# A new written-out order of instructions for a three-part float32 kernel on one core

## The chip, the cores and the metric

The kernel runs on one core of one Trainium2 chip. The metric is the device time of one execution in microseconds (us), given as the median of several runs. Five instruction streams matter: PE (TensorE, matmuls), DVE (VectorE), ACT (ScalarE), POOL (GpSimd), and SP (SyncE), which issues every DMA of this kernel. Each works through its own row of instructions strictly in the order of that row, and waits where an instruction needs something that another stream has not finished.

## What is computed

The reference is local attention with block summaries, followed by two gated feed-forward layers without a residual:

```python
def _attn_ref(q, k, v):                      # (2, 8, 768, 64) each
    k_sum = k.reshape(B, H, nb, 32, D).max(axis=3)
    v_sum = v.reshape(B, H, nb, 32, D).mean(axis=3)
    ...                                      # a window of 16 to either side, and 24 summaries
    return np.matmul(a, v_all)

def _moe_ref(x, w1, w2, w3, w_out):          # x: 1536 x 512, d_ff 1024
    h = (x @ w1) * (x @ w2) @ w3
    return h @ w_out

def _moe2_ref(x, w_in, w_out):               # d_ff 2048
    h = x @ w_in
    g = h * np.clip(h + 3.0, 0.0, 6.0) / 6.0
    return g @ w_out
```

The feed-forward weights arrive as 64-bit floats. The kernel rebuilds 32-bit floats from their two halves on the chip, and splits each into a high and a low part, so that one product of float32 accuracy is three matmuls (high by high, low by high, high by low).

## The kernel before

The work is a graph of 1997 numbered operations, built in `build` (L247). An operation is a load or store on SP, one instruction on DVE, ACT or POOL (the softmax's `inv` is three), or a group of matmuls on PE. Most copies and subtractions may run on either of two engines (`alt`, L71). Nothing decides this at run time: the table `PLAN` (L105) writes out, for PE, ACT, DVE, POOL and SP, which operations the engine does and in which order, and `Graph.in_order` (L88) only checks that the five lists together are possible and records them.

The stages, in the order of time:

- W' (`wprime`): w3 times w_out, once, so that the first layer's last two products become one. It has 16 steps. A step loads one or two tiles of 128x512 numbers (512 KB, `load`, L321), turns them into floats (`to_f32`: ACT L362, ACT L368 or DVE L371, DVE L376), splits them (`to_hi_lo`: a copy at L328 or L330, a subtraction at L387 on POOL or DVE), and gives PE four products of three matmuls each (`products`, L426), one into each of four PSUM banks. The tiles of the first step come in two halves of 128x256. The first tiles of attention (`probabilities`, `attend`, L531 to L640), and the sums over blocks (`first_k` L443, `first_v` L479, `vsum_rows` L505), are woven in. The loads of this stage go to the buffers raw0 to raw7, k to kres, q to qst, v windows to vall.
- The first layer (`ab`, `acc1`) in three blocks of 512 tokens, with the rest of attention woven in. At its side the weights w1 and w2 are converted, and later the second layer's output weights are converted and spilled to DRAM (`wo`).
- The second layer. Its first product is done by a seven-product scheme of 2x2 blocks (`half_product`, `added`, `gated`) in eight groups, with sums and differences of weights made on DVE, POOL and ACT (L826, L882, L387, L652). Sums of output weights are spilled to DRAM (`ws`).
- The last stage. Seven products of the same scheme over eight chunks each: every chunk loads 256 KB of `wo` or `ws` into half of a slot w20 to w27 (L1095), makes the high and low part of a difference of activations, and gives two products into two banks. Finished rows go from a bank through c0 to c3 to the output (L703, L1073).

A product into one bank is the chain

```python
for lhs, rhs in terms:
    for a, c in PASSES:                # L425: high*high, low*high, high*low
        nc.tensor.matmul(out=out_ap, lhsT=lhs(a), rhs=rhs(c), ...)
```

A buffer is used again as soon as its last reader is done. So an operation waits for its inputs, for the readers of the buffer that it writes, and for whatever stands before it in its engine's row.

Of the kernel before, what the change touches and what calls it, by code (L numbers as in the profile page):

```python
# [60 lines left out]
class Graph:  # L61
# [26 lines left out]
    def in_order(self, plan):  # L88
# [18 lines left out]
        33, 34, 35, 32, 49, 51, 50, 48, 58, 263, 73, 72, 74, 75, 274, 91, 89, 88, 90, 105, 106, 107, 104, 284,  # L107
        282, 122, 123, 120, 121, 286, 137, 138, 139, 292, 136, 300, 302, 153, 154, 155, 152, 304, 173, 171,
        181, 170, 183, 310, 180, 191, 318, 172, 320, 182, 192, 190, 322, 193, 200, 202, 201, 203, 210, 211,
        450, 212, 213, 458, 220, 230, 223, 460, 222, 232, 242, 462, 221, 231, 240, 241, 233, 243, 466, 465,  # L110
        475, 490, 491, 497, 485, 501, 483, 500, 496, 487, 506, 534, 540, 535, 510, 544, 519, 499, 509, 529,
        498, 508, 542, 527, 507, 541, 551, 531, 550, 552, 545, 562, 543, 553, 570, 578, 572, 577, 574, 587,
        584, 585, 586, 583, 601, 594, 593, 609, 596, 611, 595, 588, 616, 617, 625, 623, 622, 624, 613, 635,
        633, 634, 632, 627, 626, 648, 663, 670, 671, 664, 658, 673, 674, 669, 656, 681, 679, 703, 708, 710,
        680, 709, 672, 682, 711, 702, 660, 712, 687, 719, 718, 721, 695, 713, 697, 720, 742, 750, 749, 747,
        699, 748, 741, 726, 751, 736, 758, 759, 752, 757, 734, 768, 763, 738, 776, 769, 761, 774, 775, 765,
        760, 784, 786, 785, 777, 787, 778, 779, 796, 797, 806, 802, 805, 803, 804, 814, 812, 813, 807, 815,
        816, 817, 826, 825, 822, 836, 823, 824, 846, 834, 827, 832, 835, 837, 842, 845, 844, 847, 856, 855,
        854, 1051, 852, 857, 1066, 833, 843, 1072, 1053, 865, 864, 1057, 1083, 1092, 862, 1054, 1056, 1155,
        853, 863, 1055, 1145, 1068, 1078, 1153, 1147, 1087, 1163, 1162, 1161, 1173, 1160, 1148, 1170, 1171,  # L120
        1172, 1159, 1223, 1177, 1237, 1236, 1169, 1235, 1182, 1238, 1221, 1231, 1229, 1299, 1239, 1224, 1258,
        1248, 1246, 1247, 1307, 1253, 1249, 1314, 1313, 1300, 1324, 1245, 1312, 1322, 1297, 1329, 1388, 1305,
        1323, 1389, 1315, 1311, 1321, 1325, 1387, 1390, 1334, 1373, 1383, 1397, 1398, 1399, 1400, 1381, 1376,
        1391, 1451, 1375, 1401, 1405, 1464, 1463, 1449, 1465, 1466, 1410, 1457, 1459, 1467, 1527, 1452, 1475,
        1474, 1473, 1476, 1477, 1481, 1542, 1541, 1539, 1525, 1540, 1528, 1552, 1533, 1551, 1549, 1550, 1486,
        1598, 1595, 1535, 1543, 1596, 1597, 1553, 1562, 1583, 1581, 1557, 1591, 1589, 1584, 1607, 1599, 1606,
        1667, 1609, 1672, 1677, 1613, 1625, 1624, 1682, 1687, 1608, 1626, 1709, 1605, 1623, 1714, 1618, 1719,
        1666, 1708, 1713, 1718, 1630, 1629, 1723, 1728, 1733, 1628, 1671, 1676, 1738, 1681, 1686, 1691, 1696,
        1701, 1754, 1760, 1801, 1724, 1766, 1772, 1778, 1807, 1729, 1734, 1739, 1627, 1692, 1697, 1702, 1813,
# [1074 lines left out]
```

## Time and profile before

| | us |
|---|---|
| median of 3 runs | 554.68 |
| lowest and highest | 553.05, 556.45 |
| profiled execution | 554.5 |
| its span, first to last instruction | 552.7 |
| PE busy within the span | 531.0 |

The profile is one execution. Its span leaves out what lies around the instructions. An engine is counted busy while an instruction is in it; "<-" behind idle time names what ended it. Matmuls overlap in the pipeline, and their ends are modelled, so that the distance from start to start is what to read. PEclk is the granted share of TensorE's clock, 1.00 being 2.4 GHz.

### The profile page before, as it was taken

To read this page: it belongs to the slowest core of one execution; us is meant where nothing else is said; L and a number is where in the kernel's file an instruction comes from. 1 tells how busy PE (TensorE), PEld (TensorE's weight loads), DVE (VectorE), ACT (ScalarE), POOL (GpSimd) and SP (SyncE) were. 2 spreads that over 40 slices of the span, in tenths; PEclk is the share of its full clock that TensorE was granted. 3 is DMA by queue.
4 is the path that set the end of the run, shared out by engine and by line. 5 is a ranking of instruction groups with operands and counts; after the bars stand their busy time and mean duration, and the time that the engine had idled before them with its cause. 6 is when DMAs were issued, how large, how long until landed. Compare 5 with 4: busy or idle time off the path is not lost.

```text
span 552.7 us, 8430 instructions
## 1 busy us (share of the span) xinstructions
PE 531.0 (96%) x3112; PEld 430.2 (78%) x3112; DVE 437.3 (79%) x647; ACT 219.8 (40%) x365; POOL 259.7 (47%) x204
## 2 busy tenths in 40 slices
PE   2799999999999999999999999999999999999997
PEld 1477788877887877888788888888888888877885
DVE  5989999688989265497558898788989999867881
ACT  3598584273564321211425335534420352332231
POOL 0487377713521111174656235864654335656461
PEclk9999999999999999999999999999999999999999
DMA  8999597486679620001147674644653589758741
GB/s 311 399 341 326 154 320 270 128 288 195 212 265 303 242 80 30 0 1 39 42 169 236 195 272 163 219 165 132 269 177 114 196 296 377 259 167 267 234 147 57
DMA packets 54512, 111.32 MB, mean 201 GB/s; under 512 B 4792, under 2 KB 26296, under 8 KB 54472
## 3 DMA queue, kind: packets, MB, share of 16 engines
q1 hardware_dynamic: 54472, 110.79, 59.2%
q8 instruction: 24, 0.39, 0.3%
q14 instruction: 16, 0.13, 0.1%
HBM read 84.26 MB, written 26.21 MB: 200 GB/s over the span
## 4 chain that ended last, share of the span: by engine, by line
PE 81%; DVE 8%; DMA 4%; ACT 3%; POOL 2%; issue 1%; SPq 0%; DVEq 0%; POOLq 0%
PE bank L426 76%; PE bank L619 2%; PE bank L560 2%; DMA w<-ws 2%; PE bank L607 2%; DVE c L376 1%; DMA arena<-wo 1%; DMA raw<-in_wp_dram 1%; ACT bank L362 1%; ACT arena L328 1%; ACT raw L368 1%; DVE c L826 1%; POOL arena L652 1%; DVE arena L387 0%; DVE sc L570 0%
## 5 line engine op out<-in xcount | busy, mean ns | idle before, releaser
L426 PE MATMUL bank<-arena,w 128*128 128x512 f32 x1152 | 272.3, 390 | 1.9 <-DMA w<-ws 1.8
L426 PE MATMUL bank<-arena 128*128 128x512 f32 x960 | 242.3, 400 | 15.2 <-DVE arena L330 11.5
L426 PEld LDWEIGHTS bank<-arena,w 128*128 128x128 f32 x1152 | 215.2, 188 | 48.7 <-DVE arena L387 1.5
L426 PEld LDWEIGHTS bank<-arena 128*128 128x128 f32 x960 | 179.5, 191 | 56.6 <-DVE arena L330 10.8
L387 POOL TENSOR_TENSOR arena<-late_f,arena 128x512 fp32r<-128x512 f32 x28 | 39.3, 1406 | 43.9 <-ACT arena L328 16.3
L376 DVE SCALAR_TENSOR_TENSOR c<-c,raw 128x512 uint32<-128x512 uint32 x48 | 44.2, 930 | 8.5 <-ACT raw L368 7.7
L362 ACT ACTIVATE c<-raw 128x512 f32<-128x512 f32 x48 | 32.2, 674 | 44.8 <-DMA raw<-in_w_dram 36.7
L652 POOL TENSOR_TENSOR arena<-tg,arena 128x512 fp32r<-128x512 f32 x18 | 27.3, 1519 | 45.7 <-ACT arena L328 22.9
L387 POOL TENSOR_TENSOR arena<-c,arena 128x512 fp32r<-128x512 f32 (+1 forms) x25 | 32.6, 1319 | 29.6 <-DVE arena L330 16.1
L328 ACT ACTIVATE arena<-late_f 128x512 fp32r<-128x512 f32 x40 | 24.8, 628 | 51.6 <-DVE late_f L826 21.4
L387 DVE TENSOR_TENSOR arena<-late_f,arena 128x512 fp32r<-128x512 f32 x36 | 36.5, 1024 | 4.7 <-ACT arena L328 4.6
L587 POOL TENSOR_TENSOR sc<-sc,st 128x960 f32<-128x960 f32 x10 | 18.4, 1838 | 44.7 <-DVE st L584 44.7
L387 POOL TENSOR_TENSOR w<-c,w 128x512 fp32r<-128x512 f32 x17 | 25.0, 1474 | 16.8 <-ACT w L328 10.2
L368 ACT ACTIVATE raw<-raw 128x512 uint32<-128x512 uint32 (+1 forms) x46 | 30.0, 657 | 0.0
L328 ACT ACTIVATE w<-c 128x512 fp32r<-128x512 f32 x24 | 15.0, 630 | 32.9 <-PE bank L426 24.7
L669 DVE TENSOR_TENSOR tg<-ta,bank 128x512 f32<-128x512 f32 x24 | 16.3, 680 | 13.2 <-PE bank L426 6.1
L328 ACT ACTIVATE arena<-bank 128x512 fp32r<-128x512 f32 x27 | 15.7, 597 | 25.4 <-PE bank L426 16.2
L882 POOL TENSOR_TENSOR late_f<-arena 128x512 f32<-128x512 f32 x10 | 15.3, 1537 | 20.2 <-DMA arena<-wo 19.4
L387 POOL TENSOR_TENSOR raw<-c,raw 128x512 fp32r<-128x512 f32 x11 | 14.7, 1347 | 18.7 <-ACT raw L328 12.3
L826 POOL TENSOR_TENSOR late_f<-late_f,late_f 128x256 f32<-128x256 f32 (+1 forms) x14 | 15.6, 1116 | 15.4 <-DVE late_f L882 6.3
L376 DVE SCALAR_TENSOR_TENSOR c<-bank,raw 128x512 uint32<-128x512 uint32 (+1 forms) x26 | 16.6, 645 | 6.8 <-ACT raw L368 4.8
L371 DVE TENSOR_SCALAR raw<-raw 128x512 uint32<-128x512 uint32 (+1 forms) x28 | 15.7, 563 | 7.8 <-DMA raw<-in_w_dram 6.5
(88 smaller groups left out, 619.0 us busy)
## 6 DMA issues: line engine op xcount, KB each, us to landing
raw<-in_w_dram SPq DMA_DIRECT2D x48, 512.0 KB, 4.5
raw<-in_wp_dram SPq DMA_DIRECT2D x22, 512.0 KB, 9.0
wo<-raw SPq DMA_DIRECT2D x16, 512.0 KB, 3.5
arena<-wo SPq DMA_DIRECT2D x16, 512.0 KB, 4.9
ws<-arena SPq DMA_DIRECT2D x16, 512.0 KB, 3.6
w<-ws SPq DMA_DIRECT2D x32, 256.0 KB, 4.0
arena<-gj SPq DMA_DIRECT2D x24, 256.0 KB, 5.4
w<-wo SPq DMA_DIRECT2D x24, 256.0 KB, 5.1
```

The lines of the kernel that those rows point to most:

```text
L328: nc.scalar.activation(out=out, in_=in_, func=AF.Copy, scale=scale)
L362: lambda uf=uf, wf=wf: nc.scalar.activation(out=uf, in_=wf[:, :, 1], func=AF.Prelu, scale=2.0**-112, alpha=-(2.0**32)),
L368: nc.scalar.activation(out=lw, in_=lw, func=AF.Copy, scale=2.0**-29 * (1 - eps), bias=7.5 * eps - 0.5)
L371: nc.vector.tensor_scalar(out=lw, in0=lw, scalar1=29, scalar2=None, op0=ALU.logical_shift_right)
L376: lambda ci=ci, ui=ui, lw=lw: nc.vector.scalar_tensor_tensor(out=ci, in0=ui, scalar=3, in1=lw, op0=ALU.logical_shift_left, op1=ALU.bitwise ...
L387: lambda e: eng[e].tensor_tensor(out=lo(), in0=src(), in1=hi().bitcast(F32), op=ALU.subtract),
L426: nc.tensor.matmul(out=out_ap, lhsT=lhs(a), rhs=rhs(c), start=start and n == 0, stop=stop and n == 3 * len(terms) - 1, skip_group_check=skip,)
L587: lambda e: eng[e].tensor_tensor(out=s8, in0=s8, in1=wide(0), op=ALU.subtract), [("st", i2)], skeys)
L652: lambda e: eng[e].tensor_tensor(out=slot(s)[:, 1, :], in0=src_ap, in1=slot(s)[:, 0, :].bitcast(F32), op=ALU.subtract), [src_key, ("t", s, ...
L669: g.op("dve", 685, due, lambda: nc.vector.tensor_tensor(out=gf, in0=a, in1=bank[5], op=ALU.mult), [("bank", 5), ("ta", n % 2)], [("tg", n ...
L826: lambda e: eng[e].tensor_tensor(out=out(), in0=a(), in1=b(), op=op), [ka, kb], [ko])
L882: lambda e, i=i, s=s: eng[e].tensor_tensor(out=tmps[6 + i], in0=f32s(s, 0)(), in1=f32s(s, 1)(), op=ALU.add), both(s), [k])
```

## The change

Only the five lists of `PLAN` differ; the operations, their data, the functions and every buffer stay as they are. The new lists come from the same kind of planning, for which durations and hand-overs between engines were padded by a few per cent. PE and SP have the same operations in another order. Between DVE, ACT and POOL operations also change places: 171 leave DVE and 196 come to it, 100 leave ACT and 92 come, 96 leave POOL and 79 come. In the instructions that the profile counts, DVE goes from 647 to 672, ACT's operations from 364 to 356, POOL's from 200 to 183. The table is one line shorter, so that every line of the changed file stands one lower (L426 is L425).

```diff
     "pe": [
-        33, 34, 35, 32, 49, 51, 50, 48, 58, 263, 73, 72, 74, 75, 274, 91, 89, 88, 90, 105, 106, 107, 104, 284,
+        32, 35, 34, 48, 50, 51, 33, 49, 58, 263, 74, 73, 75, 72, 274, 91, 90, 89, 88, 106, 107, 105, 282, 104,
...
     "sp": [
-        20, 24, 12, 6, 8, 54, 36, 52, 0, 42, 4, 2, 56, 60, 66, 260, 82, 76, 98, 92, 271, 108, 262, 114, 289,
+        52, 12, 36, 8, 260, 20, 24, 2, 42, 0, 60, 54, 4, 56, 6, 66, 82, 76, 98, 92, 271, 108, 114, 124, 256,
```

At the start of the program, SP's row before begins with these loads. in_wp_dram holds w3 and w_out, in_vt_dram, in_kt_dram and in_q_dram v, k and q; raw0 and raw1 receive the two weight tiles of the first step of W' in halves, raw2 and raw3 those of the second step, raw7 and (again) raw0 those of the third.

```order
L321 DMA raw1_121<-in_wp_dram 128x256 x2
L321 DMA raw0_120<-in_wp_dram 128x256
L321 DMA kres_144<-in_kt_dram 128x4x272
L321 DMA raw0_120<-in_wp_dram 128x256
L321 DMA raw5_146<-in_vt_dram 128x1024
L321 DMA raw2_122<-in_wp_dram 128x512
L321 DMA raw4_145<-in_vt_dram 128x1024
L321 DMA con_166<-in_con_dram 128x608
L321 DMA raw3_123<-in_wp_dram 128x512
```

In the changed kernel SP's row begins so:

```order
L320 DMA raw4_145<-in_vt_dram 128x1024
L320 DMA raw0_120<-in_wp_dram 128x256
L320 DMA raw2_122<-in_wp_dram 128x512
L320 DMA raw0_120<-in_wp_dram 128x256
L320 DMA qst0_158<-in_q_dram 128x512
L320 DMA raw1_121<-in_wp_dram 128x256 x2
L320 DMA kres_144<-in_kt_dram 128x4x272
L320 DMA raw3_123<-in_wp_dram 128x512
L320 DMA con_166<-in_con_dram 128x608
L320 DMA raw7_148<-in_wp_dram 128x512
```

The last half that the first step needs stands behind a tile of v, a whole tile of the second step and the first q; raw3 and raw7 stand further ahead than they did.

DVE's row in the changed kernel, from its second instruction on, has the work on the second step's raw2 ahead of the last copy of the first step's c1 (before, thirteen instructions on raw1 and raw0 came first and raw2 after them):

```order
L370 TENSOR_SCALAR raw0_120<-raw0_120 128x256
L375 SCALAR_TENSOR_TENSOR c0_124<-bank4_137,raw0_120 128x256
L370 TENSOR_SCALAR raw0_120<-raw0_120 128x256
L375 SCALAR_TENSOR_TENSOR c0_124<-bank4_137,raw0_120 128x256
L386 TENSOR_TENSOR arena_119<-c0_124,arena_119 128x256
L375 SCALAR_TENSOR_TENSOR c1_125<-bank5_138,raw1_121 128x256
L329 CAST arena_119<-c1_125 128x256
L370 TENSOR_SCALAR raw2_122<-raw2_122 128x512
L375 SCALAR_TENSOR_TENSOR c2_126<-bank4_137,raw2_122 128x512
L375 SCALAR_TENSOR_TENSOR c1_125<-bank5_138,raw1_121 128x256
L329 CAST arena_119<-c2_126 128x512
L329 CAST arena_119<-c1_125 128x256
```

Two subtractions of the first step that DVE did before now stand in POOL's row.

In the last stage, the loads of `ws` chunks go into slots that PE has just finished with. SP's row before, where the load into w20 of chunk ws3 follows three output stores:

```order
L1095 DMA w24_918<-ws0_79 128x2x256
L1095 DMA w24_918<-ws2_81 128x2x256
L944 DMA gj107_110<-late_f5_2196 128x512
L1095 DMA w25_919<-ws4_83 128x2x256
L703 DMA out_0_dram<-c2_126 128x512
L703 DMA out_0_dram<-c3_127 128x512
L1048 DMA arena_119<-gj107_110 128x512
L703 DMA out_0_dram<-c1_125 128x512
L1095 DMA w20_914<-ws3_82 128x2x256
L1095 DMA w21_915<-ws5_84 128x2x256
```

The same loads in the changed kernel:

```order
L1094 DMA w20_929<-ws3_82 128x2x256
L1047 DMA arena_119<-gj017_102 128x512
L1094 DMA w21_930<-ws5_84 128x2x256
L1047 DMA arena_119<-gj107_110 128x512
L1094 DMA w21_930<-ws7_86 128x2x256
L1094 DMA w22_931<-ws9_88 128x2x256
L702 DMA out_0_dram<-c2_126 128x512
L1094 DMA w24_933<-ws0_79 128x2x256
L1094 DMA w24_933<-ws2_81 128x2x256
L702 DMA out_0_dram<-c3_127 128x512
```

The loads into w20 to w22 now stand ahead of the stores, and those into w24 behind the first of them.

PE's row before, around the two uses of w20's second half (the product into bank4 alone, and the second product of the x6 row into bank1):

```order
L426 MATMUL bank1_134<-arena_119 128x512 x3
L426 MATMUL bank4_137<-arena_119,w20_914 128x512 x3
L426 MATMUL bank4_137<-arena_119,w21_915 128x512 x3
L426 MATMUL bank6_139<-arena_119,w27_921 128x512 x3
L426 MATMUL bank4_137<-arena_119,w21_915 128x512 x3
L426 MATMUL bank4_137<-arena_119,w22_916 128x512 x6
L426 MATMUL bank4_137<-arena_119,w23_917 128x512 x6
L426 MATMUL bank1_134<-arena_119,w20_914 128x512 x6
L426 MATMUL bank4_137<-arena_119,w24_918 128x512 x3
```

PE's row in the changed kernel, around the two uses of w24 (bank6, then bank4):

```order
L425 MATMUL bank6_139<-arena_119,w24_933 128x512 x6
L425 MATMUL bank6_139<-arena_119,w25_934 128x512 x3
L425 MATMUL bank3_136<-arena_119 128x512 x3
L425 MATMUL bank1_134<-arena_119 128x512 x3
L425 MATMUL bank7_140<-arena_119,w25_934 128x512 x3
L425 MATMUL bank0_133<-arena_119 128x512 x3
L425 MATMUL bank1_134<-arena_119,w20_929 128x512 x3
L425 MATMUL bank5_138<-arena_119,w22_931 128x512 x3
L425 MATMUL bank4_137<-arena_119,w24_933 128x512 x3
```

Before, eight products stand between the end of the old use of w20's second half and the new one. In the changed kernel w24's first half has eight between its uses (the first product of the first row frees it), and w20's second half is read for the second time only later, outside the piece shown.

## Rows read from the trace of the kernel before

**Rows 1.** The page, part 1 (busy time, share, instructions) and part 4 (the chain, by line).
```profile
PE 531.0 (96%) x3112; PEld 430.2 (78%) x3112; DVE 437.3 (79%) x647; ACT 219.8 (40%) x365; POOL 259.7 (47%) x204
...
PE bank L426 76%; PE bank L619 2%; PE bank L560 2%; DMA w<-ws 2%; PE bank L607 2%; DVE c L376 1%; DMA arena<-wo 1%; DMA raw<-in_wp_dram 1%; ACT bank L362 1%; ACT arena L328 1%; ACT raw L368 1%; DVE c L826 1%; POOL arena L652 1%; DVE arena L387 0%; DVE sc L570 0%
```
**Rows 2.** Busy time in five stretches; then PEclk, DMA share, GB/s.
```profile
0.00:30.00 30.00, 15.30 (x103) 11.06 (x104) 21.59 (x38) 14.39 (x26) 8.94 (x14) 0.94 0.96 350
30.00:60.00 30.00, 29.51 (x365) 23.39 (x365) 28.40 (x44) 23.86 (x42) 19.21 (x14) 1.00 1.05 331
60.00:240.00 180.00, 179.94 (x1305) 144.42 (x1304) 136.83 (x205) 78.63 (x129) 72.04 (x57) 1.00 0.55 183
240.00:480.00 240.00, 239.18 (x1053) 196.72 (x1052) 204.42 (x302) 83.78 (x139) 125.92 (x97) 1.00 0.54 187
480.00:553.00 73.00, 67.11 (x294) 54.62 (x292) 46.09 (x62) 19.11 (x32) 33.58 (x24) 0.99 0.55 180
```
**Rows 3.** Waits of PE in the whole span: total, times, longest.
```profile
PE bank L426 <- DVE arena L330: 11.5, 2, 10.8
PE bank L426 <- DMA w<-ws: 1.8, 2, 1.1
```
**Rows 4.** Timeline of PE to 32 us: start, length, work, idle before.
```profile
10.84 5.49 PE L426 MATMUL bank<-arena 128*128 128x512 f32 x12 [10.84 <-DVE arena L330]
16.97 0.47 PE L426 MATMUL bank<-arena 128*128 128x512 f32 x1 [0.65 <-DVE arena L330]
18.23 2.79 PE L426 MATMUL bank<-arena 128*128 128x512 f32 x11 [0.79 <-POOL arena L387]
...
24.71 0.49 PE L426 MATMUL bank<-arena 128*128 128x512 f32 x1 [1.27 <-ACT arena L328]
26.08 4.37 PE L426 MATMUL bank<-arena 128*128 128x512 f32 x11 [0.87 <-POOL arena L387]
```
**Rows 5.** Timeline of ACT, 8 to 20 us: first reads of loaded tiles.
```profile
8.06 0.41 ACT L362 ACTIVATE bank<-raw 128x256 f32<-128x256 f32 x1 [2.52 <-DMA raw<-in_wp_dram]
...
13.93 0.65 ACT L362 ACTIVATE bank<-raw 128x512 f32<-128x512 f32 x1 [0.89 <-DMA raw<-in_wp_dram]
19.49 0.64 ACT L362 ACTIVATE bank<-raw 128x512 f32<-128x512 f32 x1 [4.92 <-DMA raw<-in_wp_dram]
```
**Rows 6.** Timeline of DVE, 10 to 14 us.
```profile
10.03 0.42 DVE L376 SCALAR_TENSOR_TENSOR c<-bank,raw 128x256 uint32<-128x256 uint32 x1
10.49 0.29 DVE L330 CAST arena<-c 128x256 fp32r<-128x256 f32 x1
...
11.68 0.69 DVE L376 SCALAR_TENSOR_TENSOR c<-bank,raw 128x512 uint32<-128x512 uint32 x1
...
13.42 0.68 DVE L387 TENSOR_TENSOR arena<-c,arena 128x512 fp32r<-128x512 f32 x1
```
**Rows 7.** Timeline of POOL, 5 to 17 us.
```profile
5.17 0.73 POOL L387 TENSOR_TENSOR arena<-c,arena 128x256 fp32r<-128x256 f32 x1 [4.33 <-DVE arena L330]
16.90 1.27 POOL L387 TENSOR_TENSOR arena<-c,arena 128x512 fp32r<-128x512 f32 x1 [11.00 <-DVE arena L330]
```
**Rows 8.** The page, part 5: the same subtraction on POOL and on DVE.
```profile
L387 POOL TENSOR_TENSOR arena<-late_f,arena 128x512 fp32r<-128x512 f32 x28 | 39.3, 1406 | 43.9 <-ACT arena L328 16.3
L387 DVE TENSOR_TENSOR arena<-late_f,arena 128x512 fp32r<-128x512 f32 x36 | 36.5, 1024 | 4.7 <-ACT arena L328 4.6
```
**Rows 9.** The chain of waits, 480 to 503 us.
```profile
482.19 4.82 DMA w<-ws
...
495.62 3.95 DMA w<-ws
```
**Rows 10.** The chain of waits, its piece from 272 us and its last.
```profile
272.02 46.63 PE bank L426 x204
...
548.99 0.60 ACT c L328
```

215 rows, old and new, of the table PLAN are left out of this document.

## The prediction, made before the changed kernel ran

> **What bounds the kernel now.** I read the page first: PE is busy for 531.0 of 552.7 us, DVE for 437.3, POOL for 259.7 [rows 1]. PE is the bound if its time is work and not stretched waiting. A long stretch without waits has 204 matmuls in 46.63 us, 228.6 ns each [rows 10]. The program has 2112 matmuls of this kind, so 483 us; the 1000 short ones of attention (L560, L607, L619) are three times 2% of the span in the chain of waits [rows 1], 33 us, and some 3 more ahead of it. That is about 519 us which no order can change. The other 34 us of the span are: 10.84 before the first matmul [rows 4], 3.7 from PE's last work to the end (552.7 less 548.99) [rows 10], and some 19 of waits, of a slow clock and of fixed gaps at the short matmuls. So the order can win little and lose without limit.
>
> Then I read where PE is idle, by stretch. From 60 to 480 us it misses 0.06 and 0.82 us of 420. From 0 to 30 it misses 14.7, and from 480 to 553 5.9, of which the end is 4.0 [rows 2]. The list of PE's waits says the same: 11.5 us on the first copies, nearly all of it the first wait, and 1.8 on the loads w<-ws [rows 3]. The timeline of PE puts the waits on POOL and ACT into the first 26 us [rows 4], the chain of waits the loads w<-ws near 482 and 496 us [rows 9].
>
> **The change, place by place.** The sum is made against the profiled execution, 554.5 us with a span of 552.7; it lies beside the median of the runs (554.68).
>
> *Start, to the third step of W'.* Loads come in at a steady rate here: DMA's share is 0.96 to 1.05 for 60 us [rows 2]. ACT first reads the later half of raw0 at 8.06, raw3 at 13.93, raw7 at 19.49 us, each when it lands [rows 5]; SP's row has 1.57, 3.98 and 6.08 MB up to these. From the first to the last that is 11.43 us for 4.51 MB, 2.53 us per MB. In the new row the last half of the first step ends at 2.36 MB instead of 1.57: 8.06 + 0.79 x 2.53 = 10.1 us. raw3 ends at 3.41 MB, 12.7 us (before 13.93), and the second raw0, which the third step needs, at 6.86 MB instead of 6.60, about 0.65 us later.
>
> Behind the 10.1 us stand ACT's and DVE's rows. raw1's first half lands at 2.10 MB, 9.4 us, and from there ACT has seven instructions to do, each 0.41 us for a half tile or 0.64 for a whole one [rows 5], up to about 12.0; DVE first finishes raw2's merge (0.69) at 12.3, then merges (0.42), copies a raw2 tile (0.43, estimated as 1.5 times the half tile's 0.29) and then the half tile (0.29) [rows 6]: 13.4 us for the first matmul against 10.84. POOL's subtraction of 0.73 [rows 7] allows the second matmul at 14.1. PE then has 24 matmuls of the first two steps. Before, the first twelve took 5.49 us (427 ns apart, the level of 1.2 GHz), and eleven of the next twelve 2.79 after waits of 0.65 and 0.79 [rows 4]; they ended at 21.0. With raw3 early, the second step is ready at about 17.4, before PE asks. If the low clock lasts as long after the first matmul as before (5.4 us), the 24 end at 14.1 + 4.7 + 13 x 0.229 = 21.8. Then come the short matmuls as before. The third step waits for raw0 (21.4), ACT (0.64), DVE's copy of the summary rows that now stands ahead of it, and its merge and copy: first matmul at 24.5 and, after POOL's 1.27 [rows 7], the second at 25.8. Before they were 24.71 and 26.08 [rows 4]. I take -0.3 us. The bounds: +2.6 if nothing of the late first matmul is made up, -2.0 if also the slow clock behind it goes.
>
> That slow clock is seen at 26.08: eleven matmuls take 4.37 us where eleven at 18.23 took 2.79 [rows 4], 1.6 us more, and PEclk for 0 to 30 us is 0.94 [rows 2]. Ahead of it stood 64 short matmuls and waits of 1.27 and 0.87 us. In my chain for the new order these waits are still there (0.8 and 1.1), so I keep the 1.6.
> The Trainium skill (TensorE: Matmul & The Clock Gate, HAM oscillation) says that a TensorE kept idle between groups drops back to half clock and pays the warm-up again; the row agrees, with 4.37 against 2.79 us. By that rule alone, an order that closes the gap saves 1.6 us, which is part of the fourth rival.
>
> *Rest of W', to 60 us.* PE misses 0.49 of 30 us, and DVE is busy for 28.4 of them [rows 2], so both are nearly full. Counting operations of W', attention's first tiles and the conversions of w1 and w2 at the durations of the trace, DVE gets 0.5 us more, ACT 2 more, POOL 4 less. I take 0; bounds -0.5 (all the missing time goes) and +3 (DVE's free 1.6 us does not lie where PE needs it, and about as much again is lost).
>
> *60 to 480 us.* Only 0.9 us can be won [rows 2]. What can be lost is in the hand-overs from one product through other engines to the next. I went along each in both orders with the durations of the trace, and counted the matmul work of PE's row that stands in between, 0.69 us to a product. Of 489 groups of matmuls that have such a hand-over, before has 44 with under 1 us to spare and 94 with under 2; the new order has 30 and 76. That is in favour of it, but leaves out queueing in the rows. DVE has 25 instructions more over the whole program: some 16 come from POOL and 8 from ACT, net. At unstretched durations that is about 20 us more DVE work and 26 less for POOL; half of DVE's, 10 us, falls into 240 to 480 us, where DVE is busy 204.4 of 240 [rows 2]. The 35.6 us of free time there cover it: 214.5 of 240. Part comes back, since DVE's subtraction of two SBUF tiles took 1024 ns on average beside POOL's [rows 8] against 680 for one alone [rows 6]. I take -0.3 us; bounds -0.9 and, if the cover is gone, the second rival.
> The Trainium skill (SBUF - State Buffer, on the shared port pair) says that a VectorE operation with two SBUF inputs and a GpSimd operation that reads SBUF exclude each other for the whole instruction. The 1024 against 680 ns agree, and by it DVE's extra load would be smaller than 20 us, by up to 0.34 us for each of the 17 operations that POOL loses, some 6 us; the forecast is the same, the rival less likely.
>
> *480 to 500 us.* Before, a load into w20's second half issued at 482.19 and landed 4.82 us later, another took 3.95 [rows 9], and PE waited 1.8 us in two pieces [rows 3]. SP's row had output stores ahead of the first. In the new order those loads stand ahead of the stores and their slots are free 13 us or more before the next use. One load of the same kind becomes tight: w24's first half has eight products between its uses, 8 x 0.69 = 5.5 us, against 4.0 to 4.8 for the load, behind one store. I take -1.8 + 0.4 = -1.4; bounds -1.8 and +2 (the store in front waits for a late copy).
>
> *End.* The last two banks still end with a copy (0.60 [rows 10]) and a store. I take 0, within 0.3 either way.
>
> Sum: -0.3 + 0 - 0.3 - 1.4 + 0 = -2.0, so 554.5 - 2.0 = 552.5 us, or 0.4% less. A measurement of this kernel tells about 1% from no change (5.5 us; the three runs are 3.4 apart).
>
> **The rivals.**
>
> First, no gain: new hand-overs of the same size take the place of the old. For it: the w24 load above, and that each of the sixteen steps of W' has several feeds with less than 1 us to spare. Against it: fewer tight hand-overs. Every wait that goes is replaced: 554.5 us. Chance 0.28.
>
> Second, slower: DVE becomes the bound in the second layer. The place is 240 to 480 us, the price its extra 10 us, since in the fullest parts of that stretch DVE is already busy without a break, and a subtraction that POOL did beside it now stands in DVE's row. It decides once DVE is busy for about 228 of the 240 us (95%); then PE waits for most of what came: about +8, 560.5 us. For it: DVE is the only other engine near its limit, and PE has held its pace there with hand-overs of less than 1 us. Against it: 214 is not 228. Chance 0.17.
>
> Third, a late start that is not made up: the first matmul 2.6 us later, the short matmuls behind it too, and the clock falling once more for 1.6: +4.2 and then the -1.7 of the later places, 557.0 us. For it: the first 60 us are full for DMA and DVE at once, with nothing to catch up with. Against it: raw3 comes 1.2 us earlier. Chance 0.14.
>
> Fourth, faster by over 1%: all waits of the first 26 us go (0.65 + 0.79 + 1.27 + 0.87 = 3.6), the slow clock (1.6), the 1.8 at 482 us and 0.9 between: 7.9, or 546.6 us. Against it: the third step's raw0 cannot land earlier at 2.53 us per MB. Chance 0.05.
>
> **How the numbers follow.** The forecast has 0.36, its own range 550 to 554. The second rival lies above 1% (560.2) in all but a little, and I give some of the third's mass to it: slower 0.18. Faster 0.06, from the fourth and the edge of the forecast. Same 0.76. The range goes from 549.0, below which only the fourth lies, to 560.5, the middle of the second; outside it remain about 0.05 and 0.1.
>
> **What would show it.** Right: first matmul near 13.4 us and the third step's long run of matmuls at about the same time as before; PE's waits on w<-ws below 0.7 us; PE missing under 2 us from 60 to 480; DVE about 210 to 215 us busy between 240 and 480. Wrong: PE waits on DVE rows L375 or L386 in the second layer, PEclk below 1.00 anywhere after 30 us, or a PE that reaches 60 us of the program with more than 2 us less work done than before.

## The result, and the profile of the changed kernel

The changed kernel takes 550.71 us (median of 14 runs, 548.8 to 553.96) against 555.47 us of the kernel before (14 runs on the same chip): 0.9918 of it, 95% interval 0.9892 to 0.9944. On another chip the ratio was 0.9898 (0.9874 to 0.9923). So it is 0.8 to 1.0% faster, where 0.4% was predicted. Its profiled execution took 550.11 us with a span of 548.3, 4.4 us under the profiled one before.

The page of the changed kernel (busy time, share, instructions; then the same subtraction on POOL and on DVE) answers [rows 1] and [rows 8]:

```profile
PE 528.4 (96%) x3112; PEld 429.2 (78%) x3112; DVE 454.8 (83%) x672; ACT 213.8 (39%) x357; POOL 235.9 (43%) x187
...
L386 POOL TENSOR_TENSOR arena<-late_f,arena 128x512 fp32r<-128x512 f32 x27 | 40.9, 1524 | 44.5 <-ACT arena L327 21.9
...
L386 DVE TENSOR_TENSOR arena<-late_f,arena 128x512 fp32r<-128x512 f32 x37 | 32.1, 878 | 5.3 <-ACT arena L327 5.1
```

DVE has 17.5 us more work and POOL 23.8 less. The stretches show where DVE's share of it lies (columns as in [rows 2]):

```profile
0.00:30.00 30.00, 15.69 (x169) 10.93 (x170) 21.61 (x37) 14.10 (x27) 9.87 (x15) 1.00 0.97 358
30.00:60.00 30.00, 28.56 (x296) 21.63 (x296) 26.18 (x41) 23.89 (x42) 21.44 (x15) 1.00 1.05 317
60.00:240.00 180.00, 179.56 (x1307) 144.76 (x1306) 147.87 (x218) 76.31 (x125) 63.32 (x51) 1.00 0.56 184
240.00:480.00 240.00, 240.00 (x1060) 198.70 (x1059) 210.93 (x315) 83.07 (x138) 109.20 (x87) 1.00 0.55 192
480.00:549.00 69.00, 64.63 (x286) 53.18 (x284) 48.24 (x65) 16.39 (x27) 32.06 (x21) 1.00 0.52 173
```

From 240 to 480 us PE misses nothing, with DVE at 210.9 us. PEclk is 1.00 throughout; before it was 0.94 in the first 30 us [rows 2], and one piece of 3.4 us at half clock accounts for that. The rows of the kernel before, with the same columns:

```profile
26.00:27.00 1.00, 0.92 (x3) 0.79 (x4) 0.97 (x3) 0.96 (x3) 0.63 (x2) 0.74 1.09 414
27.00:28.00 1.00, 1.00 (x3) 0.77 (x3) 1.00 (x2) 1.00 (x2) 1.00 (x1) 0.50 1.04 352
28.00:29.00 1.00, 1.00 (x4) 0.75 (x3) 0.47 (x1) 1.00 (x3) 1.00 (x2) 0.50 1.07 244
29.00:30.00 1.00, 1.00 (x4) 0.81 (x3) 0.72 (x2) 1.00 (x3) 1.00 (x2) 0.56 0.96 334
```

PEclk does not show everything: the first matmuls of either kernel begin 427 ns apart, the pace of 1.2 GHz (before, all of the first twelve [rows 4]; here most of the six in the second row of the timeline below), under a PEclk of 1.00. PE's waits over the whole span, all of the list, against [rows 3]:

```profile
PE bank L425 <- ACT arena L327: 11.5, 1, 11.5
PE bank L425 <- POOL arena L386: 1.9, 4, 0.8
PE bank L559 <- DVE vall L331: 0.8, 1, 0.8
PE bank L559 <- DVE arena L635: 0.7, 1, 0.7
PE bank L425 <- DVE arena L329: 0.5, 1, 0.5
PE bank L618 <- ACT pt L327: 0.4, 1, 0.4
```

The loads w<-ws are gone from it. All six waits lie in the first 60 us or in attention. The timeline of PE, as [rows 4]:

```profile
11.47 2.82 PE L425 MATMUL bank<-arena 128*128 128x512 f32 x4 [11.47 <-ACT arena L327]
14.69 2.70 PE L425 MATMUL bank<-arena 128*128 128x512 f32 x6 [0.40 <-POOL arena L386]
17.65 3.48 PE L425 MATMUL bank<-arena 128*128 128x512 f32 x14 [0.26 <-POOL arena L386]
20.97 0.60 PE L504 MATMUL bank<-con,vsum 128*24 128x128 f32 x4
...
24.48 0.47 PE L425 MATMUL bank<-arena 128*128 128x512 f32 x1 [0.53 <-DVE arena L329]
25.76 2.83 PE L425 MATMUL bank<-arena 128*128 128x512 f32 x11 [0.81 <-POOL arena L386]
```

The third step begins when it began before (24.71 and 26.08), but its eleven matmuls take 2.83 us instead of 4.37.

**Where the 4.4 us came from.** After the last matmuls of attention both kernels have the same 1362 matmuls of 128x512 left. The chain of waits of the changed kernel has them in one piece:

```profile
235.65 309.00 PE bank L425 x1362
...
544.67 0.60 ACT c L327
```

The chain of the kernel before begins them at the same time, but leaves PE three times on the way (256, 319 and 482 us) and once more at 496 us; two of its PE pieces are

```profile
235.69 20.64 PE bank L426 x90
...
341.70 140.49 PE bank L426 x619
```

and the loads and a third piece stand in [rows 9] and [rows 10]. From 235.69 to the last copy at 548.99 that is 313.30 us, against 309.02 now. Between these two executions all of the gain arises here, and none in the 235 us ahead, although the clock and several waits changed there.

To see that in more detail I placed every group of matmuls by the work ahead of it on PE (227.8 ns for each 128x512 matmul, attention's groups at their shortest), and took start to next start less the group's own work. "Last 1362" is from the start of the first of them to the end of PE's work. All in us, from the profiled executions:

| kernel | first matmul | extra, 0 to 10 | 10 to 100 | 100 to 250 | 250 to 455 | 455 to 475 | last 1362 start | they take |
|---|---|---|---|---|---|---|---|---|
| before | 10.84 | 9.50 | 3.83 | 4.02 | -0.16 | 2.31 | 235.62 | 313.3 |
| changed | 11.47 | 7.00 | 6.03 | 2.59 | -0.98 | -0.10 | 235.58 | 309.0 |
| changed, again (after_again) | 11.10 | 6.94 | 7.57 | 2.59 | -0.96 | -0.10 | 236.69 | 309.0 |
| start_old | 11.72 | 9.53 | 5.26 | 2.60 | -1.00 | -0.10 | 237.59 | 309.0 |
| start_new | 11.55 | 6.94 | 5.93 | 3.22 | 0.58 | 2.43 | 235.43 | 313.8 |
| start_new_fix | 11.32 | 6.96 | 5.27 | 4.66 | 0.04 | 0.84 | 236.11 | 311.6 |
| fix_load | 11.56 | 10.93 | 4.70 | 4.65 | -0.21 | 0.77 | 239.46 | 311.6 |
| last_new | 11.50 | 9.51 | 5.85 | 4.40 | 2.58 | -0.10 | 238.91 | 313.4 |
| middle_new | 11.80 | 7.93 | 5.41 | 2.60 | 9.80 | 0.38 | 236.21 | 320.3 |
| early_raw3 | 11.94 | 11.04 | 4.64 | 4.30 | -0.55 | 1.83 | 239.75 | 312.1 |
| order_only | 11.09 | 9.74 | 6.99 | 6.67 | 5.87 | 0.24 | 241.86 | 318.2 |
| engines_only | 11.95 | 10.89 | 9.35 | 7.39 | 8.14 | 2.14 | 245.62 | 322.8 |
| after_moved | 11.20 | 7.44 | 6.15 | 2.59 | -1.00 | -0.10 | 235.86 | 309.0 |
| after_moved_q | 11.66 | 6.56 | 7.64 | 2.59 | -1.00 | -0.10 | 236.93 | 309.0 |

A small negative value is a stretch that goes at less than 227.8 ns. From the third row on they are the experiments.

Against the 226.9 ns per matmul that the changed kernel holds over its last 1362, nearly all that the kernel before loses there lies at five places: 1.0 us near 271, 0.3 near 324, 0.35 near 342, 1.4 near 486 and 1.0 near 499 us; all others together have some 0.1 to 0.2. The first is the wait on ACT, the last two are the loads. The second and third stand in no list of waits. In PE's timeline (322.5 to 325 and 340 to 342.5 us) they are rows without a break, but too long: at 226.9 ns from start to start and 0.39 us for the last matmul, eleven take 2.66 us and four 1.07.

```profile
322.33 2.96 PE L426 MATMUL bank<-arena,w 128*128 128x512 f32 x11
...
341.25 1.42 PE L426 MATMUL bank<-arena 128*128 128x512 f32 x4
```

### The profile page after: what moved, and what is told of

It reads as the page before. It is cut to its first block, busy times and chain, and to the rows that moved or that the text cites. A ratio compares the mean times of both kernels' runs of the same rounds, so it can differ in the third digit from the quotient of the medians.

```text
span 548.3 us, 8416 instructions
## 1 busy us (share of the span) xinstructions
PE 528.4 (96%) x3112; PEld 429.2 (78%) x3112; DVE 454.8 (83%) x672; ACT 213.8 (39%) x357; POOL 235.9 (43%) x187
## 4 chain that ended last, share of the span: by engine, by line
PE 85%; DMA 11%; DVE 1%; ACT 1%; SPq 1%; issue 0%; DVEq 0%; ACTq 0%
PE bank L425 81%; DMA vall<-in_vw_dram 3%; DMA raw<-in_wp_dram 3%; DMA kres<-in_kt_dram 2%; DMA vall<-vall 2%; PE bank L618 2%; PE bank L606 1%; PE bank L559 1%; DMA raw<-in_w_dram 1%; SPq L320 1%; DVE c L375 0%; DVE ksum L442 0%; DVE st L590 0%; ACT pt L327 0%; ACT sc L587 0%
## 5 line engine op out<-in xcount | busy, mean ns | idle before, releaser
L425 PE MATMUL bank<-arena,w 128*128 128x512 f32 x1152 | 271.4, 390 | 0.0
L425 PE MATMUL bank<-arena 128*128 128x512 f32 x960 | 242.8, 398 | 14.0 <-ACT arena L327 11.5
L425 PEld LDWEIGHTS bank<-arena,w 128*128 128x128 f32 x1152 | 215.8, 188 | 45.3 <-issue 0.2
L425 PEld LDWEIGHTS bank<-arena 128*128 128x128 f32 x960 | 177.8, 189 | 54.7 <-ACT arena L327 11.4
L375 DVE SCALAR_TENSOR_TENSOR c<-c,raw 128x512 uint32<-128x512 uint32 x48 | 41.2, 860 | 6.4 <-ACT raw L367 5.4
L651 POOL TENSOR_TENSOR arena<-tg,arena 128x512 fp32r<-128x512 f32 x17 | 24.4, 1437 | 41.4 <-DVE arena L329 20.0
L386 DVE TENSOR_TENSOR arena<-late_f,arena 128x512 fp32r<-128x512 f32 x37 | 32.1, 878 | 5.3 <-ACT arena L327 5.1
L386 POOL TENSOR_TENSOR w<-c,w 128x512 fp32r<-128x512 f32 x12 | 17.2, 1436 | 23.0 <-ACT w L327 17.2
L386 POOL TENSOR_TENSOR raw<-c,raw 128x512 fp32r<-128x512 f32 x6 | 8.5, 1417 | 39.3 <-ACT raw L327 24.2
L938 DVE SCALAR_TENSOR_TENSOR late_f<-ta,late_f 128x512 f32<-128x512 f32 x24 | 24.0, 1002 | 0.2
L361 ACT ACTIVATE bank<-raw 128x512 f32<-128x512 f32 (+1 forms) x26 | 15.6, 600 | 18.9 <-DMA raw<-in_wp_dram 14.8
L327 ACT ACTIVATE late_f<-bank 128x512 f32<-128x512 f32 x17 | 10.1, 597 | 31.8 <-PE bank L425 31.7
L386 DVE TENSOR_TENSOR w<-c,w 128x512 fp32r<-128x512 f32 x28 | 21.1, 760 | 0.8 <-ACT w L327 0.8
L651 DVE TENSOR_TENSOR arena<-tg,arena 128x512 fp32r<-128x512 f32 x23 | 18.0, 783 | 3.8 <-ACT arena L327 3.5
```

What stands on the lines that cost most here:

```text
L327: nc.scalar.activation(out=out, in_=in_, func=AF.Copy, scale=scale)
L361: lambda uf=uf, wf=wf: nc.scalar.activation(out=uf, in_=wf[:, :, 1], func=AF.Prelu, scale=2.0**-112, alpha=-(2.0**32)),
L375: lambda ci=ci, ui=ui, lw=lw: nc.vector.scalar_tensor_tensor(out=ci, in0=ui, scalar=3, in1=lw, op0=ALU.logical_shift_left, op1=ALU.bitwise ...
L386: lambda e: eng[e].tensor_tensor(out=lo(), in0=src(), in1=hi().bitcast(F32), op=ALU.subtract),
L425: nc.tensor.matmul(out=out_ap, lhsT=lhs(a), rhs=rhs(c), start=start and n == 0, stop=stop and n == 3 * len(terms) - 1, skip_group_check=skip,)
L651: lambda e: eng[e].tensor_tensor(out=slot(s)[:, 1, :], in0=src_ap, in1=slot(s)[:, 0, :].bitcast(F32), op=ALU.subtract), [src_key, ("t", s, ...
```

## The experiments

Three theories were to be told apart. A: the gain is made at places, above all at the loads of `ws`. B: the middle, 60 to 440 us, is quieter because work was taken off POOL. C: the gain is made at the start, by the clock. All kernels do all of the computation; only `PLAN` differs. Ratios are to the kernel before on the same chip. Medians are of 12 runs where nothing else is said.

**Cutting the change by time.** Each list is taken from one kernel up to a time of its trace and from the other behind it. In PE's row the seams are:

```diff
 start_new: changed up to 62 us, then before
-        33, 34, 35, 32, 49,
+        32, 35, 34, 48, 50,
...
         318, 190, 320, 202, 183, 322, 193, 200,

 start_old: before up to 62 us, then changed
         33, 34, 35, 32, 49,
...
         320, 182, 192, 190, 202, 200, 322, 201,

 last_new: before up to 440 us, then changed
...
         1598, 1595, 1535, 1543, 1553, 1562, 1591, 1581,
```

> The new order for what had begun by 62 us in its own trace, the old order for the rest. Theory A: first matmul at 11.5 instead of 10.8 us, PE reaches 60 us of the program with about the same work done, the gain being only what the clock gives: between 0 and 1.6 us, ratio 0.997 to 1.000; the waits on w<-ws of 1.8 us and the one near 270 us are still there. Rival B: 1.000. Rival C: the whole gain, 0.992.

> The old order for what had begun by 62 us, the new order for the rest. Theory A: 2.4 + 1.4 us less, ratio 0.993, with the slow clock near 26 us as in the kernel before. Rival B: 0.992 to 0.994 too, but with PE's gain spread over 60 to 440 us and not at two places. Rival C: 1.000.

> The old order up to what had begun at 440 us, the new order for all that remains (about the last fifth). Theory A (the gain is made of places: 2.4 us at the loads w<-ws, 1.6 of slow clock near 26 us, 1.4 between 220 and 290 us): PE no longer waits for w<-ws, so 2.4 us less, ratio to before 0.996. Rival B (the gain is the quieter middle, because work was taken off POOL): 1.000. Rival C (the gain is the start, where the clock stays up): 1.000.

Measured: start_new 554.76 us, ratio 0.9972 (0.995 to 0.9993); start_old 552.16 us, 0.9937 (0.9909 to 0.9964); last_new 556.68 us, 1.0004 (0.9981 to 1.0027).

The two halves add up: 0.28% and 0.63% against 0.8 to 1.0% for the whole (start_old's seam costs one wait of 0.85 us at 64 us). The larger part is made behind 62 us, which C alone does not allow: none of start_old's 12 runs shows a granted clock of 1.00 over the span, and nine of start_new's 12 do. start_old's chain has the last part as the changed kernel does:

```profile
237.66 308.98 PE bank L430 x1362
```

and start_new keeps the old waits on the loads in its list of PE's waits:

```profile
PE bank L429 <- DMA w<-ws: 2.0, 2, 1.2
```

last_new was a miss for A as first put. The loads' wait goes (extra -0.10 at 455 to 475), yet nothing is gained, because PE waits at the seam instead. Its timeline of PE at the seam:

```profile
444.21 3.01 PE L429 MATMUL bank<-arena,w 128*128 128x512 f32 x12 [0.69 <-ACT late_f L331]
448.01 1.66 PE L429 MATMUL bank<-arena,w 128*128 128x512 f32 x6 [0.78 <-DVE late_f L917]
450.06 1.66 PE L429 MATMUL bank<-arena,w 128*128 128x512 f32 x6 [0.39 <-DVE tg L942]
```

At a seam the two orders have not done the same work in advance, so such a cut tells only about the parts away from it.

**The new middle alone** (before to 62 us, changed to 440 us, then before).

```diff
 middle_new
...
         320, 182, 192, 190, 202, 200, 322, 201,
...
```

> The old order up to 62 us, the new order from there for what had begun by 440 us in its trace, the old order for the rest. Theory A as it stands now (the gain is about 1.5 us of clock at the start, 2.4 at w<-ws, 2.5 between 60 and 440 us): the last alone, less a little at the two seams, ratio 0.995 to 0.998, with 1.8 us of waits on w<-ws. Rival B (the middle carries the gain): 0.993 or less. Rival C: 1.000.

Measured: 564.82 us (6 runs), 1.0165 (1.0127 to 1.0203), which none of the theories had. The middle itself is as in the changed kernel (2.60 at 100 to 250), but the second seam costs some 10 us. Its list of PE's waits, and its stretch 440 to 480 us, in which the clock falls too:

```profile
PE bank L430 <- DVE tg L943: 6.2, 1, 6.2
```

```profile
440.00:480.00 40.00, 32.11 (x131) 24.72 (x130) 29.40 (x39) 10.59 (x18) 13.41 (x10) 0.91 0.77 260
```

So the worth of the middle by itself was not got from this run; it is read from start_old's row of the table.

**The loads of ws alone.** In the old order the load of ws3 into w20's second half goes ahead of four instructions of SP, the load of ws11 into w22 too, and the product that frees w22 is taken earlier on PE.

```diff
 fix_load, "sp"
         1622, 1812,
+        1758,
         1636, 1638, 1654, 1634,
-        1758,
         1764, 1770, 1776,
+        1782,
         1818, 1824, 1830, 1836,
-        1782,
 fix_load, "pe"
         1691, 1696, 1701,
+        1692,
         1754, 1760, 1801,
...
         1627,
-        1692,
```

> The old order with three moves and nothing else: on SP the load of chunk ws3 into w20 goes ahead of two output stores, and the load of ws11 (w23's slot, second half of w22's neighbour) goes ahead of four other loads; on PE the one product that frees the latter's slot goes nine products forward. Theory A: PE's waits on w<-ws (1.8 us named, 2.2 from start to start) go: ratio 0.996. Rival B and rival C: 1.000.

Measured: 555.91 us, 0.9992 (0.9968 to 1.0015). The wait falls from 1.8 to

```profile
PE bank L429 <- DMA w<-ws: 0.6, 1, 0.6
```

and the last 1362 matmuls take 311.6 instead of 313.3 us, but the time does not show the 1.7 us: the profiled execution is behind by 3.8 us when they start. The interval reaches to a gain of 0.32%, 1.8 us, so this neither shows nor excludes it. The same moves were made on top of start_new, with one copy on ACT (828) three places earlier:

```diff
 start_new_fix, "act", beside the moves of fix_load
         818, 971,
+        828,
         990, 991, 875,
-        828,
```

> The new order up to 62 us, then the old order with four moves: the three of the load experiment, and on ACT the copy out of bank4 near 271 us goes ahead of the conversion work that stood before it. Theory A (places): 0.9972 for the start, less 1.5 to 2.2 us for the loads, less 0.7 for the copy: ratio 0.992 to 0.993, nearly the whole gain of the new order. Rival B (the middle gains from what the planner moved off POOL, spread over it): 0.9955 at best, since about 2 us between 60 and 440 us are not at these places.

Measured: 553.3 us, 0.9941 (0.9915 to 0.9968), against start_new's 0.9972: 0.3%, 1.7 us, and the last part takes 311.6 instead of 313.8. The intervals of the two ratios overlap, and that of start_new_fix holds A's 0.992 to 0.993 as well as B's 0.9955, so the times do not decide; the table does, at the place of the loads. At 455 to 475 us of work the extra time falls from 2.43 to 0.84 us, and from 2.31 to 0.77 in fix_load. So these moves are worth about 1.6 us there, of the 2.4 that the changed kernel wins. That leaves 2.6 us to the changed kernel's 309.0. Start to start, 0.9 of them are still at the loads (489 and 500 us), 0.6 near 276, 0.3 near 303 and 0.4 near 342 us: again places, and no loss spread over the middle as B has it.

**Order or engines.** order_only has PE's and SP's rows of the changed kernel and gives every operation of DVE, ACT and POOL to the engine that had it before, in the order in which the changed kernel starts them. engines_only is the reverse.

```diff
 order_only, "dve", against the changed kernel
-        53, 10, 11, 14, 15, 17, 23, 28, 38, 39,
+        53, 10, 11, 14, 15, 16, 17, 23, 18, 28, 38, 39,
...
 engines_only, "dve", against the kernel before
-        23, 28, 27, 30, 31, 10, 11, 16, 17, 14, 15,
+        23, 28, 27, 30, 10, 11, 17, 14, 15, 38, 39,
...
```

> The new order, with every operation on the engine that did it before: PE and SP have the new rows, and on DVE, ACT and POOL the operations stand in the time order of the new kernel's trace. Theory A: the rows of PE and SP carry the start and the w<-ws places, so 3 to 4 us of the gain stay unless the old engines queue badly in the new rows: ratio 0.993 to 0.998, no waits on w<-ws, and POOL's operations as long as before (1406 ns for the subtraction). Rival B: the gain goes, 1.000 or more.

> The old order, with every operation on the engine that the new lists give it: PE and SP have the old rows. Theory A: no gain at the start or at w<-ws, the operations that went to other engines come at odd places of their rows: 1.000 to 1.010. Rival B: 0.995 or less, with PE's excess between 60 and 440 us down by 2 us.

Measured: order_only 566.29 us (6 runs), 1.0162 (1.0121 to 1.0204); engines_only 573.89 us (6 runs), 1.0302 (1.0261 to 1.0343). Either half of the change alone makes the kernel slower. The waits of order_only, for example, are many and small, and on every engine (first rows behind the start):

```profile
PE bank L429 <- POOL arena L390: 2.9, 4, 0.9
PE bank L429 <- DVE late_f L333: 2.3, 2, 1.7
PE bank L563 <- DVE arena L639: 1.5, 2, 1.4
PE bank L429 <- ACT arena L331: 1.5, 2, 1.2
```

Both lie outside what A had given (0.993 to 0.998, and 1.000 to 1.010). B, in the form that taking work off POOL helps by itself, is not borne out: engines_only has that and is the slowest. Both kernels are joins, ordered by the times of a trace; a plan made anew for either half was not tried. So they show that the engines pay together with the order that was made for them, not what either half could give.

**The start.** early_raw3 takes one thing of the new start into the old order: raw3 is loaded earlier, and DVE works on it earlier.

```diff
 early_raw3, "sp"
         54, 36,
+        42,
         52, 0,
-        42,
 early_raw3, "dve"
         38, 39,
+        44, 45, 46,
         53, 41, 55,
-        44, 45, 46,
```

> The old order with raw3's load two places earlier on SP (3.15 MB instead of 3.98 up to its end, so about 2.1 us earlier) and the three instructions on it ahead of two sums on DVE. Theory A on the clock (it falls when waits stand near the short matmuls of the first attention tiles): PE's waits of 0.65 and 0.79 us near 17 us go, the one in front of the third step stays; the clock still falls in most executions: 0.997 to 1.000. Rival C (the clock stays up if the first two steps run without a gap): the clock stays at 1.00 in most executions, and the ratio is 0.996 or less.

Measured: 555.7 us, 1.0005 (0.9984 to 1.0026). The first two steps now run without a gap (24 matmuls in one row of PE's timeline, 8.44 us from 11.94), but the wait moves to the sums of v, and in the profiled execution the clock is lower for longer:

```profile
PE bank L508 <- DVE vsum L482: 1.9, 1, 1.9
```

```profile
0.00:60.00 60.00, 44.48 (x453) 34.28 (x454) 47.53 (x76) 37.35 (x65) 28.15 (x27) 0.91 1.00 335
```

None of its 12 runs shows a granted clock of 1.00 over the span. So C's condition, two steps without a gap, is met, and the clock falls all the same.

**The W' stage of the changed kernel.** after_moved takes its waits there away: a copy of the summary rows (59) goes from DVE to ACT, an attention product (292) behind two of W' (138, 136), and a copy (80) ahead of a conversion (93). after_moved_q loads q (289) one place earlier as well. They ran in different batches, so the changed kernel ran once more beside the second.

```diff
 after_moved, against the changed kernel
 "act"
         62, 64,
+        59,
         67, 83,
...
+        80,
         93,
-        80,
 "dve"
         254,
-        59,
         253,
 "pe"
         137,
-        292,
         138, 136,
+        292,
 after_moved_q, "sp", beside them
         256,
+        289,
         130,
-        289,
```

> The new order with three moves in W': the copy of the summary rows (L508) goes from DVE to ACT, ahead of the read of the second raw0, as in the old order; the scores of the third tile (292) go behind the two products that followed them on PE; one copy on ACT (80) goes ahead of one read (93). Theory A: the new order's waits at 22.65 (0.77 us), in front of the third step (0.5) and at 42.5 us (0.7) shrink or go, 1.0 to 1.5 us less than the new order: ratio to before 0.989 to 0.990, against 0.9918. A rival that these waits only move on (DVE and DMA set the pace of W'): 0.992.

> after_moved with the load of q (SP 289) issued one place earlier, ahead of instruction 130, so that W' at 80 to 90 us no longer waits for that load (0.8 us in after_moved). If the waits of the W' stage are delays by themselves, 0.988 to 0.990 (1 to 2 us under after_again). If that stage goes at VectorE's pace, the wait comes back on VectorE's tg at about 90 us as it did in after_moved (1.8 us) and the time is that of after_again within 0.3%.

> The changed kernel once more, unaltered, as the measure for the version with moved places on the same chip: 0.992 of the kernel before (0.989 to 0.995), 550 to 551 us. If the quieter middle and the missing loads' wait are what it gains, PE again has under 0.5 us more than its products at 200 to 250 us and at 455 to 475 us of product time, whatever the clock at the start does. If the clock at the start were all of it, an execution with the slow piece at about 25 us would stand at 554 or above.

Measured (6 runs each): after_moved 550.0 us, 0.9899 (0.9871 to 0.9927); after_moved_q 550.6 us, 0.9906 (0.9881 to 0.9931); the changed kernel beside it 550.98 us, 0.9898 (0.9874 to 0.9923). None of the three can be told from another. In after_moved the extra time at 10 to 45 us of work falls from 4.08 to 2.66 us, and comes back as a wait on DVE's tg at 90 us. The repeat of the changed kernel shows that this wait is no fault of the moves. It has it as well, in an execution that was 1.3 us ahead at 78 us:

```profile
PE bank L425 <- DVE tg L668: 2.0, 1, 2.0
```

Why DVE is late there is seen in its timeline, first of the repeat:

```profile
84.53 1.58 DVE L375 SCALAR_TENSOR_TENSOR c<-c,raw 128x512 uint32<-128x512 uint32 x1
...
87.23 1.45 DVE L375 SCALAR_TENSOR_TENSOR c<-c,raw 128x512 uint32<-128x512 uint32 x1
```

and POOL's of the same execution:

```profile
84.27 1.29 POOL L386 TENSOR_TENSOR arena<-c,arena 128x512 fp32r<-128x512 f32 x1 [1.83 <-ACT arena L327]
86.85 1.28 POOL L386 TENSOR_TENSOR arena<-c,arena 128x512 fp32r<-128x512 f32 x1 [1.29 <-ACT arena L327]
```

Each merge starts just behind a subtraction of POOL and ends 0.55 us after that one's end (84.27 + 1.29 = 85.56, and 84.53 + 1.58 = 86.11; 88.13 and 88.68). In the first execution of the same kernel the first merge started 0.2 us ahead of POOL, and took its usual time; POOL's two subtractions took 1.7 on average:

```profile
85.52 0.68 DVE L375 SCALAR_TENSOR_TENSOR c<-c,raw 128x512 uint32<-128x512 uint32 x1
...
87.31 0.68 DVE L375 SCALAR_TENSOR_TENSOR c<-c,raw 128x512 uint32<-128x512 uint32 x1
```

```profile
85.73 3.41 POOL L386 TENSOR_TENSOR arena<-c,arena 128x512 fp32r<-128x512 f32 x2 [1.85 <-ACT arena L327]
```

The Trainium skill (SBUF — State Buffer, SBUF: two separate sides) says that of a VectorE operation with two SBUF inputs and a GpSimd operation that reads SBUF, the one that starts first has the shared port pair for its whole instruction and the other is blocked. These rows agree, to the constant 0.55 us behind POOL's end. In this stage POOL's place in time therefore decides what DVE costs, and a start that is 1 us earlier can meet it worse.

after_again also bears on C. Its one execution with a granted clock of 0.995 over the span took 551.69 us, and one of the five at 1.00 took 551.67. The 14 runs of the result speak the other way: the eight at 1.00 have a median of 549.93 us, the five at 0.997 and 0.994 one of 553.64. But the clock is not the whole gain: the five runs of the kernel before at 1.00 that ran beside start_new have a median of 555.27 us.

## Why the prediction came out as it did

The direction, the class (same within 1%) and the range (549.0 to 560.5) held; the size was half of what was measured.

*Start, to the third step: -0.3 us forecast.* The times of the third step held (24.5 and 25.8 forecast, 24.48 and 25.76 measured; 24.10 and 25.38 in the repeat). The load of raw3 came as counted, 12.98 against 12.7 us, and DVE's last copy of the first step too, at 13.44 against 13.4. ACT's timeline, and DVE's:

```profile
12.98 0.65 ACT L361 ACTIVATE bank<-raw 128x512 f32<-128x512 f32 x1 [0.92 <-DMA raw<-in_wp_dram]
```

```profile
12.71 0.73 DVE L329 CAST arena<-c 128x512 fp32r<-128x512 f32 x2
```

Two steps failed. The first matmul came at 11.47, not 13.4: I let the first product wait for the last half tile of c1, and only the second one, into bank3, needs it. It is the fourth matmul of the timeline's first row (11.47 + 2.82 = 14.29, less the 0.7 of one at the low clock, is 13.6). And the slow clock of 1.6 us, which I kept because the waits of 1.27 and 0.87 ahead of it stay, was gone: 2.83 us for the eleven matmuls, with waits of 0.77, 0.53 and 0.81 in front.
The Trainium skill (TensorE: Matmul & The Clock Gate, HAM oscillation) lets the clock fall after idle time. These rows do not bear out that closing a gap was needed: the sum of the waits is the same (2.11 against 2.14 us), in smaller pieces.
Of the 20 runs of the changed kernel 13 show a granted clock of 1.00 over the span, of start_new's 12 nine, of start_new_fix's 12 six, of after_moved's and after_moved_q's 12 five. With the first 62 us of before it is 7 of 80 for the kernel before beside the experiments, none of 12 each for start_old and fix_load, none of middle_new's six and four of 12 for last_new. So the new first 62 us do keep the clock up more often. Which part of them does it stays open: early_raw3 did not.

*Rest of W': 0 forecast, -0.5 to +3.* PE loses there most of what the start had won: 5.16 us extra at 10 to 60 us of work, 4.25 in the repeat, against 2.71. The forecast's sum to 60 us, -0.3, came out as +0.6 and -0.8, near it by luck: the first 10 us of work have 2.5 us less extra time than before, and the next 50 have 2.45 more (1.54 in the repeat). The upper bound had DVE's free time lie in the wrong places; the last experiments show besides that PE, once ahead, waits later for DVE and for loads, so that what it wins early is not kept.

What the slow clock costs stays open. In the kernel before (the runs beside start_new) five runs at 1.00 had a median of 555.27 us and 13 at 0.997, which is what one slow piece of 3.4 us makes of the mean, 555.10; but the 14 at 0.995 and less had 557.49, and in the changed kernel 3.7 us lie between the runs at 1.00 and those at 0.997 and less. That the clock makes these runs longer is not shown.
Still the new start is worth something: 0.28% by start_new. The profiled execution before was one of its better starts: the last 1362 matmuls began at 235.6 us, and at 237.6 and 238.9 in start_old and last_new, which have its first 60 us unchanged.

*60 to 480 us: -0.3 forecast, at best -0.9.* This is the step that failed most. Outside the loads, extra time fell by 1.43 at 100 to 250 and by 0.82 at 250 to 455: -2.2 us, of which the list of waits of before had named one, 0.7 us on ACT at 272 us. I had read "only 0.9 us can be won" from PE's busy time. A wait that is shorter than the overlap of two matmuls (0.39 us long in this trace, 0.227 from start to start) does not show as idle there; start to start shows it, as near 324 and 342 us above, and the waits that are listed cost more than the list says: 2.4 us for the loads instead of 1.8, 1.0 for ACT instead of 0.7. The floor of "519 us which no order can change" was off too: its 228.6 ns is the length of a piece in the chain over its count of matmuls [rows 10]. From start to start that stretch, 272.02 to 318.70 us, has 227.7 ns, some small waits included. The piece of 619 above has 227.0 ns, and the 1362 have 226.9, so the floor was 2112 x 1.7 ns = 3.6 us too high.

*480 to 500 us: -1.4 forecast, bounds -1.8 to +2.* Right in mechanism, short in size: -2.4 us from start to start, where the list of waits names 1.8. The cost that I had set against it, a tight load into w24, was nil. PE's timeline answers [rows 9]:

```profile
481.23 25.10 PE L425 MATMUL bank<-arena,w 128*128 128x512 f32 x110
```

from 481 to 506 us there is no break.

*End: 0.* Held: 3.7 us from PE's last work to the end of the span, as before.

*The rivals.* DVE as the bound did not come: 210.9 busy us of 240 (214.5 counted, 228 to decide), and PE at 240.00. The two parts of DVE's cost were seen in advance, more operations and shorter ones: its subtraction fell from 1024 to 878 ns, while POOL's, fewer by one, grew from 1406 to 1524. A late start not made up (557.0) did not come, since the start was not late. "Every wait that goes is replaced" is true of the first 100 us only, and there after_moved shows it. The fourth rival's parts came half: the clock and the w<-ws waits went, the waits of the first 26 us did not.

What stays open is why the new middle has no waits. The extra time at 100 to 250 us repeats to 0.01 us in all six executions of kernels with the new middle (2.59 or 2.60), and the last 1362 matmuls take 309.0 in the five that also have the new end; the six with the old middle scatter from 3.22 to 4.66 there. That fits an order made with a margin at every hand-over. It was not shown, since the margin could not be taken out with the order kept; the five places say where the old order lost, not why the new one loses nowhere.

## What to carry to other kernels

Read small losses of a full engine from start to start, against the longest undisturbed run of the same instruction, and not from its idle time or its list of waits: here the list named 2.5 us (1.8 on loads, 0.7 on ACT) of the 4.3 that could be won behind attention. An order written out per engine and the assignment to engines are one object: either half alone, as joined here, cost 1.6 and 3.0%, and a cut between two good orders cost up to 10 us at the seam. And in a stage that goes at the pace of loads or of another engine, removing a wait moves it; look for the next operation that paces the stage before counting the gain.

## What was not expected of the hardware

- Which of DVE and POOL starts first decides the length of both, by 0.2 us of chance: a merge of 0.68 us took 1.58 and 1.45 behind POOL's subtraction, and POOL's subtraction 1.7 on average instead of 1.3 us behind DVE's.
- An undisturbed PE repeats its pace closely: 309.00, 309.01, 308.98, 308.97 and 308.98 us for 1362 matmuls in five executions of four kernels.
- A piece of 3.4 us at half clock need not show in the time: 555.10 us for the 13 runs of the kernel before at 0.997, 555.27 for the five at 1.00. The 14 runs with a clock of 0.995 and less had 557.49; why is not shown.
- PEclk reads 1.00 while the first matmuls of either kernel go at 427 ns, the pace of 1.2 GHz.
